# Six merges of probability tiles per unit in another order, and one direct part in the row sums

## The chip, the cores and the metric

The kernel runs on one core of a Trainium2 chip. The metric is the device time of one execution in microseconds (us).

## What is computed

Two identical layers on 2048 tokens of width 1024, in float32. Each is attention with 32 heads of 32 columns, then a routed feed-forward on 8 tokens:

```python
x = x + A(layernorm(x)); x = x + B(layernorm(x))          # twice
# A: q, k, v = split(x @ wqkv); p = softmax(q @ k.T * 32**-0.5); (p @ v) @ wo
# B(y): r = y @ w_r; the 8 tokens with the largest r get
#    y + sigmoid(r) * ((silu(y @ w_gate) * (y @ w_up)) @ w_down), the others y
```

The change lies in the softmax of A: the sums of the exponentials over the keys, by which the outputs are divided.

## The kernel before

Attention of a layer goes through 32 units (NU). A unit is a group of 4 heads (8 groups, NG) and a chunk of 512 queries (4 chunks, QC). Each unit has 16 steps (NT), one for each block of 128 keys. Steps are counted through the layer as `s`; within a unit they are called `kt`.

In a step TensorE makes, in this order: a first half of a row of products of q and k for the row maxima, 25 steps ahead of their use (`pre_mm`, L706; VectorE reduces them, L714); the scores of 128 keys by 512 queries for 4 heads, in two halves (`scores`, L721, into the two PSUM tiles `pre`); the other half of `pre_mm`; and the values matmul of the tile before (`pv_step`, L1043). ScalarE turns the scores into exponentials (L1112). They go to a tile P of 128 x 2048 float32, 1 MB; "tile k" is the P of step k of a unit. P has 9 buffers (PB). In the last 24 steps of a layer no products for maxima are left, and the steps go in threes.

The sum over the keys has two levels. First, the 16 tiles of a unit are added elementwise, in one of three ways:

- `merge(u, a, b)` (L1056): GpSimd issues a DMA that adds tile b onto tile a in SBUF. It needs the exponential of b, and the values matmul of a must have read a. Tile b is free when the DMA has landed.
- `acc_add` (L1053): GpSimd adds a tile into an accumulator `acc` of the unit (the first add takes two tiles). In the last units VectorE does some of it.
- a direct part: the tile is left as it is.

Then `sum_mm` (L1063) makes 8 matmul instructions with a matrix of ones for each part, that is for each direct tile and for the accumulator, which add up over the 128 rows. ScalarE copies the result (L1073), and SyncE stores it.

Each engine has its own queue in the order of the program, and an instruction at the head that waits holds up all behind it. `emit(s, where)` puts the work on the sums into the program, by lists written by hand: in the lists before, `(8, 6)` of MERGED is the merge of tile 7 onto tile 6, put at the end of step 8. Numbers of 16 and more lie in the steps of the next unit. The place only sets the order in the queue; the work starts when the engine gets there and what it needs is done. The sum is put at step 22, the middle of step 6 of the next unit (`SUM_AT`), after the values matmul of tile 5. SyncE loads q for later units at the start of a unit, and keys in the first two units of a group, values in the third, for the next group (`queue_loads`).

A buffer of P that has been released is given to the next new tile; before the first exponential of the tile ScalarE waits for the last use of what lay in the buffer.

Of the kernel before, what the change touches and what calls it, by code (L numbers as in the profile page):

```python
# [19 lines left out]
NT = S // 128  # L20
# [3 lines left out]
NU = NG * QC  # L24
# [9 lines left out]
PB = 9  # L34


MERGED = ((2, 0), (8, 6), (11, 8), (13, 10), (15, 12))
ADDED = ((5, 3), (6, 0), (9, 5), (12, 4), (14, 6), (15, 8), (16, 10), (20, 12))
FIRST = 2
DIRECT = (14, 15)  # L40
LAST_DIRECT = (13, 14, 15)


# [4 lines left out]
KEYS_AT[3, 3] = slice(3 * 512, S)  # L48

ON_DVE = 9


def unit_events(left):

    if left == 0:
        return [(k + 1, "mid", 1, "add", (k, 0 if k == 1 else None, True)) for k in range(1, NT) if k not in LAST_DIRECT]
    ev = [(at, "end", 0, "merge", (k, k + 1)) for at, k in MERGED]
    ev += [(at, "end", 1, "add", (k, FIRST if at == ADDED[0][0] else None, left == 1 and at >= ON_DVE)) for at, k in ADDED]  # L60
    return ev + [(SUM_AT, "mid", 5, "sum", ())]


EVENTS = [unit_events(i) for i in range(3)]


@with_exitstack
def tile_kernel(ctx, tc, x, wqkv, wo, w_r, w_gate, w_up, w_down, out):
# [29 lines left out]
    def ps_st():  # L98
        return banks["now"][1].tile([128, 512], F32, name="st", bufs=1 if banks["wide"] else 3)

    def ps_pre():
        return psum.tile([128, 1024], F32, name="pre", bufs=2)

    def ps_pv():
        return psum.tile([128, 512], F32, name="pv")
# [544 lines left out]
    def layer(n, src, dst, prev=None, following=None):  # L650
# [93 lines left out]
        with ExitStack() as pst:  # L744
# [209 lines left out]
            for k, (c, wb, i) in enumerate(steps):  # L954
# [26 lines left out]
                at = b - (1, 8)[c == 0]  # L981
# [31 lines left out]
        with sbuf(f"at{n}", bufs=2) as aw:  # L1013
            KS[1] = aw.tile([128, 2, 2, S], F32R, name="ks1", bufs=1)
            P, PV, ACC = {}, {}, {}
# [41 lines left out]

            def sum_mm(u):
                p = ps_st()
                parts = [P[u * NT + k] for k in (DIRECT if u < NU - 1 else LAST_DIRECT)] + [ACC.pop(u).rearrange("p (h c) -> p h c", h=4)]  # L1060
                for i, a in enumerate(parts):
                    for h in range(4):
                        pe.matmul(p[32 * h:32 * h + 32, :], ones32, a[:, h, :], start=(i == 0),  # L1063
                                  stop=(i == len(parts) - 1), tile_position=(0, 32 * h))
                return p
# [12 lines left out]
            def sum_out(u):  # L1078
                store_sum(u, sum_mm(u), aw.tile([128, 512], F32, name="sm", bufs=1))
# [13 lines left out]
            def emit(s, where):  # L1093
                u, kt = divmod(s, NT)
                todo = []
                for back in (1, 0):
                    v = u - back
                    if 0 <= v < NU:
                        todo += [(kt + NT * back, pri, fn, args, v) for (k, pos, pri, fn, args) in EVENTS[min(NU - 1 - v, 2)]
                                 if k == kt + NT * back and pos == where]  # L1100
                for k, _, fn, args, v in sorted(todo, key=lambda e: (-e[0], e[1])):
                    fns[fn](v, *args)

            for i in range(4):
# [11 lines left out]
            def rest_of_step(s):  # L1116
                u, kt = divmod(s, NT)
                pr = pre_rows[s + LEAD] if s + LEAD < NS else None
                emit(s, "mid")
                if pr and pr[1] == 15:  # L1120
                    nm_combine(pr[0])
                if (s + LEAD) % NT == 0 and NT <= s + LEAD - NT < NS:
                    nm_row((s + LEAD) // NT - 1)
                emit(s, "end")
                if s == NS + 1:
                    shared["sum"] = sum_mm(NU - 1)
                if s == NS - 20:
                    shared["first"] = aw.tile([128, 512], F32, name="sm", bufs=1)[:, 0:256]
                    sum_load(shared["first"], 0)
                if s == NS - 17:  # L1130
                    recip(shared["first"], 0)
                if s < NS and kt == 0:
                    queue_loads(u)
                    if u == NU - QC:
                        loads.extend((load_wo, a) for a in range(KD))
                if s == (NU - QC) * NT + 1:
                    right.close()
                    shared["wor"] = ExitStack()
                    wop = shared["wor"].enter_context(sbuf(f"wor{n}", side="right"))
                    shared["WOR"] = wop.tile([128, KD, D], F32, name="wor", bufs=1)  # L1140
                if loads:
                    f, *args = loads.pop(0)
                    f(*args)
# [42 lines left out]
        if True:  # L1186
# [81 lines left out]
            for t in range(NT - 2 if n else NT):  # L1268
                oh, ol = OT.pop(t)
                p = ps_pre()  # L1270
# [60 lines left out]
        if n:  # L1331

            parts = ffn.first_rows(rcols)
            waste = ps_pre()
            p = [[waste[:, h] for h in halves], [ps_st(), ps_pv()]]
            (ah, al), (bh, bl) = (OT.pop(t) for t in (NT - 2, NT - 1))
            both = range(2)
            todo = [(i, x, wol, a, both) for i, x in ((0, ah), (1, bh)) for a in range(KD)]
# [99 lines left out]
```

## Time and profile before

| | |
|---|---|
| median of 3 runs | 4543.79 us (4541.69 to 4547.17) |
| the profiled execution | 4545.36 us |
| its span, first to last instruction | 4543.6 us |
| mean granted TensorE clock | 0.996 |
| GpSimd adds into `acc` (L1053) | 422 of 4830 ns, and 62 first ones of 4761 ns |
| merges (L1056) | 310, 1024 KB each, 8.9 us from issue to landing (median) |
| exponentials (L1112) | 2016 of 1022 ns |

The profile is of one execution. An engine's busy share counts its own instructions, without waits. The chain of waits goes back from the last instruction: from each step to what released it, or to the instruction before it on its engine. PE is TensorE's matmul, PEld its weight loads, DVE is VectorE, ACT is ScalarE, POOL is GpSimd, SP is SyncE. A row of a timeline gives the start and the length in us, the engine, the line, the operation, the tile written and those read, how many were joined in the row, and in brackets the idle time of the engine ahead of it with what ended it.

### The profile page before, as it was taken

To read this page: it belongs to the slowest core of one execution; us is meant where nothing else is said; L and a number is where in the kernel's file an instruction comes from. 1 tells how busy PE (TensorE), PEld (TensorE's weight loads), DVE (VectorE), ACT (ScalarE), POOL (GpSimd) and SP (SyncE) were. 2 spreads that over 40 slices of the span, in tenths; PEclk is the share of its full clock that TensorE was granted. 3 is DMA by queue.
4 is the path that set the end of the run, shared out by engine and by line. 5 is a ranking of instruction groups with operands and counts; after the bars stand their busy time and mean duration, and the time that the engine had idled before them with its cause. 6 is when DMAs were issued, how large, how long until landed. Compare 5 with 4: busy or idle time off the path is not lost.

```text
span 4543.6 us, 73545 instructions
## 1 busy us (share of the span) xinstructions
PE 4497.7 (99%) x29241; PEld 2686.0 (59%) x29241; DVE 3156.8 (69%) x4975; ACT 2426.5 (53%) x2574; POOL 3169.1 (70%) x1239
## 2 busy tenths in 40 slices
PE   9999999999999999999999999999999999999998
PEld 7888755555555555548877786554555555555583
DVE  2211588888888888886522225888888888888763
ACT  3322266767676767670222222776767676767600
POOL 4444378989888889835633343898989898889252
PEclk9999999999999999999999999999999999999998
DMA  6757477777777768759698774777768677777598
GB/s 206 209 174 204 135 170 152 174 153 164 162 167 155 173 143 180 169 131 241 183 319 276 253 208 126 168 161 161 170 144 183 148 166 161 167 155 180 145 275 327
DMA packets 329719, 833.62 MB, mean 183 GB/s; under 512 B 43996, under 2 KB 160732, under 8 KB 280206
## 3 DMA queue, kind: packets, MB, share of 16 engines
q1 hardware_dynamic: 275454, 476.43, 35.8%
q0 software_dynamic: 45248, 325.67, 35.4%
q10 hardware_dynamic: 8672, 26.81, 2.3%
q8 instruction: 230, 3.77, 0.3%
q14 instruction: 115, 0.94, 0.1%
HBM read 384.34 MB, written 119.47 MB: 111 GB/s over the span
## 4 chain that ended last, share of the span: by engine, by line
PE 94%; DMA 2%; DVE 2%; issue 1%; POOL 1%; ACT 0%; SPq 0%; ACTq 0%; POOLq 0%; DVEq 0%
PE pv L1043 22%; PE pre L721 21%; PE st L839 17%; PE st L706 16%; PE pre L839 5%; PE pre L1283 5%; PE st L1063 4%; PE pv L549 1%; PE pre L706 1%; PE pv L839 0%; DMA ord<-rd 0%; PE pre L808 0%; DMA wraw<-in_A_wqkv_dram 0%; DVE acc L1053 0%; PE third L721 0%
## 5 line engine op out<-in xcount | busy, mean ns | idle before, releaser
L714 DVE TENSOR_REDUCE nm<-st 128x1 f32<-128x512 f32 x3916 | 2433.6, 684 | 374.7 <-PE st L706 368.8
L1112 ACT ACTIVATE P<-pre 128x1024 f32<-128x1024 f32 x2016 | 1955.2, 1022 | 704.2 <-PE pre L721 515.6
L1053 POOL TENSOR_TENSOR acc<-acc,P 128x2048 f32<-128x2048 f32 x422 | 2038.4, 4830 | 84.3 <-DMA P<-P 74.7
L721 PE MATMUL pre<-q,ks 64*128 64x512 f32 (+1 forms) x8064 | 1117.8, 395 | 1.7 <-ACT P L1112 1.7
L1043 PE MATMUL pv<-P,v 128*32 128x512 f32 x8192 | 1088.4, 605 | 4.5 <-DMA v<-vd 4.5
L706 PEld LDWEIGHTS st<-ks,q 64*128 64x128 f32 x3916 | 546.5, 184 | 906.8 <-DVE nm L714 765.3
L706 PE MATMUL st<-ks,q 64*128 64x512 f32 x3916 | 982.8, 470 | 0.4
L721 PEld LDWEIGHTS pre<-q,ks 64*128 64x128 f32 (+1 forms) x8064 | 765.2, 186 | 162.1 <-ACT P L1112 27.0
L1056 POOL DMA_DIRECT2D P<-P x310 | 294.2, 949 | 279.2 <-PE st L706 184.6
L854 DVE TENSOR_TENSOR lo<-st,hi 128x512 fp32r<-128x512 f32 x128 | 88.4, 691 | 528.0 <-ACT hi L853 507.9
L774 POOL TENSOR_TENSOR ohl<-wraw,ord 128x2048 fp32r<-128x2048 f32 (+1 forms) x54 | 222.5, 4124 | 308.4 <-ACT ord L769 292.7
L774 POOL TENSOR_TENSOR wl<-wraw,wh 128x2048 fp32r<-128x2048 f32 (+1 forms) x54 | 222.6, 4126 | 303.3 <-ACT wh L773 284.4
L853 ACT CAST hi<-st 128x512 fp32r<-128x512 f32 x128 | 75.4, 589 | 490.9 <-PE st L839 488.6
L1043 PEld LDWEIGHTS pv<-P,v 128*32 128x32 f32 x8192 | 163.3, 108 | 265.4 <-issue 258.2
L1053 POOL TENSOR_TENSOR acc<-P 128x2048 f32<-128x2048 f32 x62 | 295.2, 4761 | 11.0 <-ACT P L1112 11.0
L1283 PE MATMUL pre<-woh,ohl 128*128 128x512 f32 x960 | 223.4, 390 | 1.7 <-DVE pre L1316 0.9
L168 POOL TENSOR_TENSOR rs<-mv,eps_c 128x1 f32<-128x1 f32 x64 | 29.2, 456 | 264.7 <-DVE mv L166 264.7
L1283 PEld LDWEIGHTS pre<-woh,ohl 128*128 128x128 f32 x960 | 179.6, 188 | 42.1 <-ACT ohl L1214 2.1
L839 PE MATMUL st<-xh,wh 128*128 128x512 f32 x512 | 201.2, 393 | 0.0
L839 PE MATMUL st<-xh,wl 128*128 128x512 f32 x512 | 199.3, 389 | 0.0
L839 PE MATMUL st<-xl,wh 128*128 128x512 f32 x512 | 199.2, 389 | 0.0
L1214 ACT CAST ohl<-ord 128x1024 fp32r<-128x1024 f32 x32 | 33.6, 1051 | 272.1 <-DVE ord L1205 81.7
(389 smaller groups left out, 4069.0 us busy)
## 6 DMA issues: line engine op xcount, KB each, us to landing
P<-P POOLq DMA_DIRECT2D x310, 1024.0 KB, 8.9
wraw<-in_A_wqkv_dram SPq DMA_DIRECT2D x96, 1024.0 KB
q<-qh SPq DMA_DIRECT2D x256, 128.0 KB
ks<-kh SPq DMA_DIRECT2D x112, 256.0 KB
fw<-in_B_w_down_dram SPq DMA_DIRECT2D x17, 1024.0 KB
vd<-vn SPq DMA_DIRECT2D x32, 512.0 KB
qh<-hi SPq DMA_DIRECT2D x64, 256.0 KB
ql<-lo SPq DMA_DIRECT2D x64, 256.0 KB
```

The costliest lines, as they stand in the source:

```text
L706: pe.matmul(ps[b], Q[u][rows, i, 0, qt * 128:(qt + 1) * 128], KS[(u // QC) % 2][rows, i, 0, j * 512:(j + 1) * 512], start=True, stop=True, ...
L714: dve.tensor_reduce(NM[u][:, j, 2 * i + b:2 * i + b + 1, qt], ps[b], axis=AX.X, op=OP.max, negate=True)
L721: pe.matmul(p[:, b * 512:(b + 1) * 512], KS[(u // QC) % 2][rows, i, slot, kt * 128:(kt + 1) * 128], Q[u][rows, i, slot, :], start=(slot == ...
L774: pool.tensor_tensor(wl[:, sl], raw[:, sl], wh[:, sl].bitcast(F32), op=OP.subtract)
L839: pe.matmul(p, *pair(a, l, r), start=(a == 0 and k == 0), stop=(a == KD - 1 and k == 2))
L854: dve.tensor_tensor(lo, p, hi.bitcast(F32), op=OP.subtract)
L1043: pe.matmul(PV[u][32 * h:32 * h + 32, :], V[g][:, kt, 32 * h:32 * h + 32], P[s][:, h, :], start=(kt == 0), stop=(kt == NT - 1), tile_posit ...
L1053: (dve if on_dve else pool).tensor_tensor(o, a, P[u * NT + k].rearrange("p h c -> p (h c)"), op=OP.add)
L1056: pool.dma_start(P[u * NT + a], P[u * NT + b], accum_op=OP.add)
L1063: pe.matmul(p[32 * h:32 * h + 32, :], ones32, a[:, h, :], start=(i == 0), stop=(i == len(parts) - 1), tile_position=(0, 32 * h))
L1112: act.activation(P[s][:, 2 * i:2 * i + 2, :].rearrange("p h c -> p (h c)"), p, AF.Exp, scale=SCALE)
L1283: pe.matmul(p[:, bl], l[:, a, :], r[a][:, bl], start=(k == 0 and a == 0), stop=(k == 2 and a == KD - 1))
```

## The change

The lists of merges and adds are written anew, as one list with fractions that set the order within a step. There are six merges instead of five: 1 onto 2, 3 onto 4, 8 onto 7, 10 onto 9, 12 onto 13, 15 onto 14. The accumulator takes, in this order, 0 and 5, then 6, 2, 4, 11, 7, 9, 13: eight adds, as before. Tile 14 is the one direct part; before, 14 and 15 were. The last unit but one has a list of its own, with three merges, one GpSimd add and ten adds on VectorE, and tile 15 direct. The last unit stays as it was, with 13, 14 and 15 direct. Where the lists of two units meet in a step, the smaller fraction now goes first; before, the older unit did.

```diff
-MERGED = ((2, 0), (8, 6), (11, 8), (13, 10), (15, 12))
-ADDED = ((5, 3), (6, 0), (9, 5), (12, 4), (14, 6), (15, 8), (16, 10), (20, 12))
-FIRST = 2
-DIRECT = (14, 15)
+SUMS = (
+    (3, "merge", 2, 1), (5, "merge", 4, 3), (6, "add", 0, 5), (7, "add", 6), (9, "merge", 7, 8), (9.5, "add", 2), (11, "merge", 9, 10),
+    (11.5, "add", 4), (12, "add", 11), (14, "merge", 13, 12), (14.5, "add", 7), (16, "merge", 14, 15), (16.5, "add", 9), (19.5, "add", 13))
+DIRECT = (14,)
+
+BEHIND_SUMS = (
+    (3, "merge", 2, 1), (5, "merge", 4, 3), (6, "add", 0, 5), (7, "vadd", 6), (8, "vadd", 2), (9.5, "vadd", 9), (10, "merge", 8, 7), (11, "vadd", 4),
+    (11.5, "vadd", 10), (12, "vadd", 11), (13, "vadd", 12), (14, "vadd", 8), (15, "vadd", 13), (16, "vadd", 14))
+BEHIND_DIRECT = (15,)
 LAST_DIRECT = (13, 14, 15)
...
-ON_DVE = 9
...
-    ev = [(at, "end", 0, "merge", (k, k + 1)) for at, k in MERGED]
-    ev += [(at, "end", 1, "add", (k, FIRST if at == ADDED[0][0] else None, left == 1 and at >= ON_DVE)) for at, k in ADDED]
+    ev = []
+    for at, what, k, *other in (SUMS, BEHIND_SUMS)[left == 1]:
+        args = (k, *other) if what == "merge" else (k, *(other or [None]), what == "vadd")
+        ev.append((int(at), "end", at % 1, "merge" if what == "merge" else "add", args))
     return ev + [(SUM_AT, "mid", 5, "sum", ())]
...
-                parts = [P[u * NT + k] for k in (DIRECT if u < NU - 1 else LAST_DIRECT)] + [ACC.pop(u).rearrange("p (h c) -> p h c", h=4)]
+                parts = [P[u * NT + k] for k in (LAST_DIRECT, BEHIND_DIRECT, DIRECT)[min(NU - 1 - u, 2)]] + [ACC.pop(u).rearrange("p (h c) -> p h c", h=4)]
...
-                for k, _, fn, args, v in sorted(todo, key=lambda e: (-e[0], e[1])):
+                for k, _, fn, args, v in sorted(todo, key=lambda e: (e[1], -e[0])):
                     fns[fn](v, *args)
```

## The prediction

> **What bounds the kernel now.** I read the busy shares first, then the chain of waits, then one unit of the attention stage (layer 0, the unit whose first values matmul starts at 941.16) on TensorE, ScalarE and GpSimd.
>
> ```profile
> PE 4497.7 (99%) x29241; PEld 2686.0 (59%) x29241; DVE 3156.8 (69%) x4975; ACT 2426.5 (53%) x2574; POOL 3169.1 (70%) x1239
> PE 94%; DMA 2%; DVE 2%; issue 1%; POOL 1%; ACT 0%; SPq 0%; ACTq 0%; POOLq 0%; DVEq 0%
> ```
> The second line is the chain that ended last: TensorE carries 94% of it. So work taken from TensorE's queue in the attention stage shortens the kernel, as long as nothing makes TensorE wait instead. The stretches of that unit (length, then busy time of PE, PEld, DVE, ACT, POOL, the granted clock, the DMA share) say how near the others are:
>
> ```profile
> 941.16:986.93 45.77, 45.77 (x345) 23.17 (x344) 40.12 (x67) 32.08 (x35) 39.84 (x14) 1.00 0.78 167
> 951.16:961.16 10.00, 10.00 (x82) 4.44 (x80) 7.26 (x13) 6.34 (x7) 6.29 (x2) 1.00 0.02 4
> 971.16:986.93 15.77, 15.77 (x120) 8.29 (x112) 14.48 (x24) 11.62 (x13) 14.43 (x6) 1.00 1.05 225
> ```
> One unit takes 45.77 us, and TensorE is busy for all of it. GpSimd (39.84) and VectorE (40.12) are close behind. The DMA engines are full at the unit's end (1.05) and idle around its sum (0.02).
>
> **The term that goes.** The chain inside the unit (start, us, what) and the groups of instructions (count | busy us, mean ns | idle before):
>
> ```profile
> 954.73 1.00 PE pv L1043 x8
> 955.73 2.58 PE st L1063 x24
> 958.30 0.43 PE st L706 x2
> ```
> ```profile
> L1063 PE MATMUL st<-P,ones 128*32 128x512 f32 x1040 | 123.3, 592 | 0.0
> L1063 PE MATMUL st<-acc,ones 128*32 128x512 f32 x512 | 66.7, 592 | 2.0 <-DVE acc L1053 2.0
> ```
> The sum of a unit is 24 matmul instructions, 8 for each of its three parts: tile 14, tile 15, the accumulator. It stands on the chain with 2.58 us, so a part costs 2.58 / 3 = 0.86. By busy time a part costs 123.3 / (1040 / 8) = 0.95; I take 0.86, since neighbouring matmuls overlap and the chain counts only what each adds, and keep 0.95 as the other end. The change drops one part in every unit but the last of a layer: 31 x 2 = 62 parts. 62 x 0.86 = 53.3 us (58.9 by the other end).
>
> **What it costs GpSimd.** Let t = 0 be 941.16, where the values matmul of tile 0 starts.
>
> ```profile
> 941.16 1.07 PE L1043 MATMUL pv<-P,v 128*32 128x512 f32 x8
> 942.50 1.10 PE L721 MATMUL pre<-q,ks 64*128 64x512 f32 x8
> 943.86 1.07 PE L1043 MATMUL pv<-P,v 128*32 128x512 f32 x8
> 959.93 1.06 PE L1043 MATMUL pv<-P,v 128*32 128x512 f32 x8
> ```
> ```profile
> 942.81 0.87 POOL L1056 DMA_DIRECT2D P<-P  x1 [0.46 <-PE st L706]
> 943.43 4.88 POOL L1053 TENSOR_TENSOR acc<-acc,P 128x2048 f32<-128x2048 f32 x1
> 947.98 4.87 POOL L1053 TENSOR_TENSOR acc<-P 128x2048 f32<-128x2048 f32 x1
> 952.93 4.60 POOL L1053 TENSOR_TENSOR acc<-acc,P 128x2048 f32<-128x2048 f32 x1
> 961.58 0.87 POOL L1056 DMA_DIRECT2D P<-P  x1 [4.06 <-PE st L706]
> 966.98 0.92 POOL L1056 DMA_DIRECT2D P<-P  x1
> 972.40 0.96 POOL L1056 DMA_DIRECT2D P<-P  x1
> 977.80 1.01 POOL L1056 DMA_DIRECT2D P<-P  x1
> ```
> A step is 943.86 - 941.16 = 2.70. The fourth TensorE row is the values matmul of tile 6, the first after the sum (t = 18.77). A merge is issued 1.65 after the values matmul of its destination starts (942.81 - 941.16; 961.58 - 959.93). From a merge to the next add are 0.62, from merge over one add to merge 5.40 (961.58 to 966.98), from add to add 4.55 to 4.95. A merge with two adds behind it so takes 0.62 + 4.95 + 4.78 = 10.35, where 4.78 is 5.40 - 0.62.
>
> Both orders have eight adds per unit; the new one has six merges for five: + 0.62 for GpSimd. The unit becomes 45.77 - 0.86 = 44.91. GpSimd's new order, in t:
> - Merge 2<-1 needs the values matmul of tile 2 (5.40): 5.40 + 1.65 = 7.05. Behind it in GpSimd's queue waits the add of 13 of the unit before, the last into its accumulator; it ends at 12.45. TensorE wants that accumulator for the second part of the sum, at 955.73 - 941.16 + 0.86 = 15.4: 2.9 to spare.
> - Merge 4<-3: ready at 10.80 + 1.65 = 12.45, reached at 12.45. Adds 0+5 and 6.
> - Merge 7<-8 at 22.80 (ready near 22.3), add 2; merge 9<-10 at 28.20, adds 4 and 11; merge 13<-12 at 38.55 (ready 38.5), add 7; merge 14<-15 at 43.95, add 9 until 49.35.
> - The next unit's 2<-1 is due at 44.91 + 7.05 = 51.96: GpSimd idles 2.6 us per unit. It keeps up, with all its idle time at that one merge. Cost on the path: none while eight adds do not grow by 2.6 us together.
>
> VectorE's 40.12 of 44.91 leaves it hidden. The sixth merge is one more DMA of 1 MB per unit; by the windows above the DMA engines are free around the sum, which is where 2<-1 and 4<-3 now move.
>
> **What it costs the buffers.** A released P buffer goes to the next new tile in the order in which the last uses stand in the program; it is no fixed ring. By that order the new program gives tile 7 the buffer of 1, tile 9 that of 3, tile 3 of the next unit that of 12, tile 6 of the next that of 15. These four are set free by a merge's landing. All buffers that an add sets free come at least 5 us early (tile 2: add over at 28.2, its buffer wanted by tile 14 near 36). When the exponentials start (ScalarE):
>
> ```profile
> 940.53 1.94 ACT L1112 ACTIVATE P<-pre 128x1024 f32<-128x1024 f32 x2 [0.27 <-PE pre L721]
> 954.03 1.94 ACT L1112 ACTIVATE P<-pre 128x1024 f32<-128x1024 f32 x2 [0.76 <-PE pre L721]
> 959.28 1.94 ACT L1112 ACTIVATE P<-pre 128x1024 f32<-128x1024 f32 x2 [0.33 <-PE pre L721]
> 964.70 1.94 ACT L1112 ACTIVATE P<-pre 128x1024 f32<-128x1024 f32 x2 [0.76 <-PE pre L721]
> 983.63 1.94 ACT L1112 ACTIVATE P<-pre 128x1024 f32<-128x1024 f32 x2 [0.79 <-ACT P L1112]
> 991.73 1.94 ACT L1112 ACTIVATE P<-pre 128x1024 f32<-128x1024 f32 x2 [0.77 <-PE pre L721]
> ```
> They are tiles 1, 6, 7, 9, and 0 and 3 of the next unit. Less 0.86 for those behind the sum, tile 7 starts at t = 17.26, tile 9 at 22.68, tile 3 at 49.71; tile 6 of the next unit at 12.87 + 44.91 = 57.78. So the merges may take, from issue to landing: 2<-1 10.2 us (17.26 - 7.05), 4<-3 10.2 (22.68 - 12.45), 13<-12 11.2 (49.71 - 38.55), 14<-15 13.8. Today the tightest has 16.5 (merge at 1.65, exponential of tile 7 at 18.12). A late exponential costs TensorE nothing for the first 0.5: tile 1 is done at 942.47, and the half of the scores that needs it starts at about 942.50 + 0.55.
>
> Landings over all 310 merges (min/median/max), and of the single ones issued at 942.81, 961.58, 972.40 and 977.80:
>
> ```profile
> DMA to landing us min/median/max: 6.9/8.9/14.6
> DMA to landing us min/median/max: 9.0/9.0/9.0
> DMA to landing us min/median/max: 7.8/7.8/7.8
> DMA to landing us min/median/max: 12.2/12.2/12.2
> DMA to landing us min/median/max: 14.5/14.5/14.5
> ```
> 7.8 is a merge with little beside it, 9.0 one beside the loads of q that start with the unit, 12.2 and 14.5 two merges 5.40 apart beside the loads of keys, in the full stretch. The nearest rows for 2<-1 and 4<-3, which lie just behind the loads of q and in the empty stretch, are 7.8 and 9.0: they land at 14.9 to 16.1 and 20.3 to 21.5, in time. For 13<-12 the next merge ahead is 10.35 before it instead of 5.40, so its transfer need not queue behind another: I take 9.0 (in time), with 14.5 as the bad end.
>
> The Trainium skill ("DMA: Bandwidth & Descriptors", Anatomy of one DMA) gives 2.0 us plus the bytes at 436 GB/s, an estimate of 4.4 us for 1 MB. The trace disagrees: no merge here lands before 6.9. By the page's figure every merge would be twice as early as needed and the landing rival below would have no chance.
>
> **The end of a layer.** The last unit but one gets ten VectorE adds for six.
>
> ```profile
> L1053 DVE TENSOR_TENSOR acc<-acc,P 128x2048 f32<-128x2048 f32 x34 | 77.6, 2291 | 32.9 <-DMA P<-P 28.8 <-POOL acc L1053 2.0
> 1997.51 4.51 DVE acc L1053 x2
> ```
> Four more at 2.29 are 9.2 us per layer; VectorE waits for merges there for 28.8 / 2 = 14.4 us per layer, which the three merges of the new order mostly avoid, so they fit. The second row is on the chain: the last add of that unit stands behind two or three of the last unit's on VectorE, and the sum waits for it (the 2.0 us in the group of L1063 above). In the new order that add comes at step 16, ahead of them: - 2.0 us for both layers, or 0 if VectorE is late.
>
> **Sum.** Profiled execution 4545.4 (span 4543.6) - 53.3 - 2.0 = 4490.1. It lies 1.6 above the median of the runs, 4543.8; so 4488.5 in their terms.
>
> **The rivals.**
> 1. *Late landing of 13<-12 in some units.* For: today's fourth merge takes 14.5 in a unit that loads keys (28 units: two of four in each group, but for the last group of a layer). Against: the wider spacing. If it took 12.2 to 14.5 there, tile 3 would be 0.5 to 2.8 late beyond the slack, 1.65 in the middle: 46 us, most of the gain: 4535. Milder forms lie between 4500 and 4535; with the units that load values it could be 4545. Chance 0.13.
> 2. *Slower: 2<-1 and 4<-3 land late in every unit.* Place: exponentials of tiles 7 and 9. For: 2<-1 comes 8 us behind 14<-15, which shares the DMA engines with the loads of q. It decides from 10.2 + 0.5 + 0.86 = 11.6 us of landing on. At 12.2 the unit loses 0.64 net, 40 us in all: 4584. Against: the stretch after t = 10 has a DMA share of 0.02. Chance 0.07.
> 3. *Slower: the buffers go round as a ring of nine.* Tile 0 of the next unit (983.63, t = 41.61 in the new unit) would wait for the add of 7, over at 43.95: 2.34 - 0.5 late, less 0.86, 1.0 per unit: 4605. I read the order otherwise. Chance 0.04.
> 4. *GpSimd becomes the bound.* This needs adds longer by 2.6 / 8 = 0.33 us.
>
> ```profile
> L1053 POOL TENSOR_TENSOR acc<-acc,P x422: 4565/4891/5387, 588.8 to 4209.6; 128x2048 f32<-128x2048 f32 x141
> ```
> A mean of 5.2 would add 0.37 x 8 - 2.6 = 0.3 per unit, 20 us: 4509. Against: adds in the full stretch took no more than 5.00. Chance 0.05.
>
> That the change drops less than it says can be excluded: the list of direct parts of all but the last unit has one entry.
>
> **The numbers.** My forecast, 4488.5, has 0.71. Its own range is 4482 (a part at 0.95) to 4500. The range of 8 in 10 takes in rival 4 and the milder half of rival 1: 4480 to 4522. What a measurement here tells from no change is about 0.2%, 9 us. Faster: 0.71 + 0.05 + 0.07 of rival 1 = 0.83. Slower: rivals 2 and 3 and a little of 1, 0.12. Same: 0.05.
>
> **What would show it.** Right: the sum on the chain at 1.72 us with 16 matmuls, L1063 at 544 instead of 1040 on P, units of 44.9 us, GpSimd waiting only for TensorE at 2<-1, and ScalarE never waiting for a merge. Wrong: "ACT P" waiting for DMA P<-P or for POOL acc (rivals 1 to 3), TensorE waiting for the accumulator at the sum, or GpSimd without a gap (rival 4).

## The result and the profile after

The changed kernel takes 4505.08 us (median of 4 runs, 4503.45 to 4506.12), the kernel before 4543.88 beside it (4541.69 to 4547.17). The ratio is 0.9912, with a 95% interval of 0.9899 to 0.9924. So 38.8 us are gone, of 55.3 forecast. The profiled execution took 4506.12 (span 4504.2).

The busy shares and the chain that ended last, from the page of the changed kernel:

```profile
PE 4448.4 (99%) x28745; PEld 2674.4 (59%) x28745; DVE 3175.5 (71%) x4983; ACT 2426.1 (54%) x2574; POOL 3214.2 (71%) x1293
PE 93%; DMA 3%; DVE 2%; issue 1%; POOL 1%; ACT 0%; SPq 0%; ACTq 0%; POOLq 0%; DVEq 0%
```

TensorE has 496 instructions fewer (29241 - 28745), which is 62 parts of 8, and still carries the chain; the share of DMA on it went from 2% to 3%. The sums of two units on the chain (start, us, what), and GpSimd over one unit whose first values matmul starts at 934.90:

```profile
904.51 1.72 PE st L1066 x16
949.48 1.72 PE st L1066 x16
```
```profile
941.97 0.88 POOL L1059 DMA_DIRECT2D P<-P  x1 [2.56 <-PE st L709]
942.58 4.88 POOL L1056 TENSOR_TENSOR acc<-acc,P 128x2048 f32<-128x2048 f32 x1
947.36 0.95 POOL L1059 DMA_DIRECT2D P<-P  x1
957.50 0.89 POOL L1059 DMA_DIRECT2D P<-P  x1
962.66 1.19 POOL L1059 DMA_DIRECT2D P<-P  x1
973.39 0.88 POOL L1059 DMA_DIRECT2D P<-P  x1 [0.26 <-PE st L709]
978.53 1.20 POOL L1059 DMA_DIRECT2D P<-P  x1
```

A sum is 1.72 instead of 2.58. The next one starts 949.48 - 904.51 = 44.97 later; over most of the layer this period is 44.93, and in the kernel before it was 45.80 (both worked out from the starts of the sums). The merges come 7.07, 12.46, 22.60, 27.76, 38.49 and 43.63 after the start of the unit.

The same unit and its second quarter, as stretches (length, then busy time of PE, PEld, DVE, ACT, POOL, the granted clock, the DMA share, GB/s):

```profile
934.90:979.84 44.94, 44.94 (x338) 22.90 (x337) 40.11 (x67) 32.11 (x35) 41.96 (x15) 1.00 0.95 200
944.90:954.90 10.00, 10.00 (x82) 4.84 (x79) 8.02 (x15) 6.43 (x8) 9.92 (x4) 1.00 0.94 195
```

TensorE is busy without a gap. But the DMA engines went from 0.78 to 0.95 of a unit, and the stretch 10 to 20 us behind its start, which had a share of 0.02, now has 0.94.

Up to the last units of a layer all is as forecast. Then, once in each layer, comes a unit with a period of 54.80 (the first) and 54.14 (the second). TensorE at the first of them:

```profile
1893.77 1.04 PE L1066 MATMUL st<-acc,ones 128*32 128x512 f32 x8
1899.08 0.76 PE L709 MATMUL st<-ks,q 64*128 64x512 f32 x1 [4.27 <-DMA q<-qh]
1902.18 0.76 PE L709 MATMUL st<-ks,q 64*128 64x512 f32 x1 [2.34 <-DMA sd<-sm]
```

In brackets is TensorE's idle time. The products that wait are the first for the row maxima of the layer's last unit; what they need is that unit's q, which SyncE loads only in steps 0 to 5 of the unit in which this happens, the last but two. The second wait is put down to a store of the sums, which these products don't read. In the second layer the trace names q for both waits, 3.92 us and then

```profile
4128.42 0.76 PE L709 MATMUL st<-ks,q 64*128 64x512 f32 x1 [2.57 <-DMA q<-qh]
```

The periods are 9.87 and 9.21 longer than 44.93: 19.1 us in the profiled execution. This is the loss that the forecast doesn't have. The gain falls short by only 16.5 us, because the end of a layer gained more than forecast (below), and because the stretch from the last sum of the first layer to the first sum of the second, in which the change drops one part only, also differs from run to run (859.7 us in the kernel before, 855.2 here, 855.2 to 860.1 in the other runs with five or six merges).

SyncE's issues ahead of the stall, in the kernel before and then in the changed one:

```profile
1889.66 7.47 SPq L96 DMA_DIRECT2D wor<-in_A_wo_dram  x7
1902.55 6.02 SPq L96 DMA_DIRECT2D q<-qh  x4
1910.50 5.55 SPq L96 DMA_DIRECT2D q<-ql  x2
```
```profile
1859.28 6.51 SPq L99 DMA_DIRECT2D wor<-in_A_wo_dram  x7
1878.14 2.13 SPq L99 DMA_DIRECT2D q<-qh  x4
1880.37 4.16 SPq L99 DMA_DIRECT2D q<-ql  x2
```

In both, seven loads of wo go out together, after the row-maxima transfers let SyncE go on, and the q loads follow. In the kernel before, the products that need this q start without a wait, 4 us after its last issue ended (1910.50 + 5.55). In the changed kernel the last issue ended at 1880.37 + 4.16 = 1884.53, some 10 us before TensorE wanted this q, and that was not enough. The products of the kernel before:

```profile
1919.06 1.04 PE L1063 MATMUL st<-acc,ones 128*32 128x512 f32 x8
1920.03 0.50 PE L706 MATMUL st<-ks,q 64*128 64x512 f32 x2
```

The stretches from the issues of wo on, before and then after:

```profile
1885.00:1905.00 20.00, 20.00 (x154) 10.70 (x151) 18.27 (x30) 14.39 (x16) 19.40 (x7) 1.00 1.03 249
1905.00:1921.00 16.00, 16.00 (x126) 7.74 (x124) 12.60 (x22) 10.29 (x11) 13.33 (x4) 1.00 0.91 265
```
```profile
1860.00:1880.00 20.00, 20.00 (x152) 10.26 (x146) 18.31 (x30) 14.97 (x16) 19.62 (x8) 1.00 1.02 268
1880.00:1900.00 20.00, 15.57 (x117) 7.40 (x113) 12.80 (x22) 10.28 (x11) 17.36 (x6) 0.95 1.05 248
```

Both are full when wo goes out. Before, the engines have room again (0.91) while q comes in; after, they are still full (1.05). Whether it is this that makes q late, the experiments have to tell.

### The profile page after: what moved, and what is told of

It is laid out like the page before. It is cut to its first block, busy times and chain, and to the rows that moved or that the text cites. A ratio compares the mean times of both kernels' runs of the same rounds, so it can differ in the third digit from the quotient of the medians.

```text
span 4504.2 us, 72867 instructions
## 1 busy us (share of the span) xinstructions
PE 4448.4 (99%) x28745; PEld 2674.4 (59%) x28745; DVE 3175.5 (71%) x4983; ACT 2426.1 (54%) x2574; POOL 3214.2 (71%) x1293
## 3 DMA queue, kind: packets, MB, share of 16 engines
q0 software_dynamic: 53312, 384.39, 43.2%
q1 hardware_dynamic: 275454, 476.43, 35.5%
## 4 chain that ended last, share of the span: by engine, by line
PE 93%; DMA 3%; DVE 2%; issue 1%; POOL 1%; ACT 0%; SPq 0%; ACTq 0%; POOLq 0%; DVEq 0%
PE pv L1046 23%; PE pre L724 21%; PE st L842 17%; PE st L709 16%; PE pre L842 6%; PE pre L1286 4%; PE st L1066 2%; PE pv L552 1%; PE pre L709 1%; DMA ord<-rd 1%; PE pv L842 1%; PE pre L811 0%; DMA q<-qh 0%; PE third L724 0%; DVE ord L1208 0%
## 5 line engine op out<-in xcount | busy, mean ns | idle before, releaser
L1056 POOL TENSOR_TENSOR acc<-acc,P 128x2048 f32<-128x2048 f32 x420 | 2052.0, 4886 | 9.4
L1059 POOL DMA_DIRECT2D P<-P x366 | 364.3, 995 | 268.3 <-PE st L709 244.3
L1056 POOL TENSOR_TENSOR acc<-P 128x2048 f32<-128x2048 f32 x62 | 307.4, 4957 | 0.0
```

The lines of the kernel that those rows point to most:

```text
L1056: (dve if on_dve else pool).tensor_tensor(o, a, P[u * NT + k].rearrange("p h c -> p (h c)"), op=OP.add)
L1059: pool.dma_start(P[u * NT + a], P[u * NT + b], accum_op=OP.add)
```

## The experiments

Each was timed beside the kernel before on the same chip, which took 4547.30 us on one chip (wo at `NU - 2`, five merges, old order with six), 4545.81 on another (the last two runs) and 4543.80 on a third (the others). So runs on different chips are compared by their ratios. The edits are to the changed kernel unless said otherwise.

**Move the loads of wo.** First to the last unit but one, behind the last loads of q:

```diff
-                    if u == NU - QC:
+                    if u == NU - 2:
```

> The changed kernel, with the eight loads of wo queued at the start of the last unit but one of a layer instead of the first unit of the last group. Theory A (the loads of q for the last unit come late, because eight loads of 512 KB and six merges a unit fill the DMA engines just ahead of them, and TensorE waits for q at the first products for maxima of the last unit): the wait of some 9 to 10 us goes in both layers, 4505 becomes 4485 to 4488, and no period between sums is over 46 us. Theory B (the stall at the layer's end comes from the new list of the last unit but one, through VectorE): nothing changes, 4503 to 4507.

4493.31 us (4490.22 to 4496.69); ratio 0.9876 (0.9861 to 0.9892). The wait for q is gone and every period is 44.93 until the layer's end. But the last period but one is 39.88 in the first layer and 36.63 in the second, for 34.91 and 34.95 in the changed kernel. TensorE and SyncE there:

```profile
1960.20 1.34 PE L724 MATMUL pre<-q,ks 33*128 33x512 f32 x2 [1.31 <-DMA q<-nmx]
```
```profile
1945.36 7.46 SPq L99 DMA_DIRECT2D nmx<-nmr  x4
1958.21 1.18 SPq L99 DMA_DIRECT2D q<-nmx  x2
```

The row maxima of the last unit, which go out to DRAM and back into q, now stand behind wo. So the move took away the wait for the loads of q and made a new one, for the row maxima. The same move in the kernel before:

> The kernel before, with the same move of the loads of wo. Theory A: with five merges a unit q came just in time, so there is nothing to gain: 4542 to 4546. Theory B: the same. If instead it gains 5 us or more, the kernel before was paying for that collision too, and the changed kernel's gain is smaller by that than the direct part's price says.

4554.68 us (4550.41 to 4557.23); ratio 1.0013 (1.0004 to 1.0022), so some 6 us slower than before, which the expectation didn't have. Its trace shows no wait of TensorE for the row maxima; the last period but one is longer in both layers (38.37 and 39.58 us for 37.19 and 36.93, between the starts of the accumulator's part), and what makes it so is not shown. Now one unit earlier, so that the row maxima don't stand behind wo, in the changed kernel and in the kernel before:

```diff
-                    if u == NU - QC:
+                    if u == NU - 3:
```

> The changed kernel, with the loads of wo queued one unit later than in the changed kernel, behind the last unit's loads of q (the last unit but two). Theory A (the missing time is q coming late behind the loads of wo): every period between sums 44.9 us up to the last two, the last ones 34.9 and 23.8 as in the changed kernel, no wait for DMA at the products for maxima: 20 us under the changed kernel, 4484 to 4488, a ratio to the kernel before near 0.987. If wo only collides with something else there, as it did with the row maxima's way through memory when it was put into the last unit but one, the gain is less than 17.

> The kernel before with the same move. Theory A: nothing to gain, ratio 0.998 to 1.002, periods of 45.8. The difference to the run with the changed lists is then what the change brings without the collision: the forecast says 55 us.

Changed kernel with the move: 4489.24 us (4488.67 to 4490.55); ratio 0.9881 (0.9866 to 0.9896). Kernel before with the move: 4542.57 (4541.32 to 4547.55); ratio 0.9999 (0.999 to 1.0008). SyncE in the first of the two:

```profile
1879.52 4.48 SPq L99 DMA_DIRECT2D q<-qh  x4
1884.04 2.49 SPq L99 DMA_DIRECT2D q<-ql  x2
1905.55 5.47 SPq L99 DMA_DIRECT2D wor<-in_A_wo_dram  x7
```

The loads of q go out alone, wo 20 us later. All periods are 44.93 up to the last two (34.95 and 23.75). The expectation's mark for a second collision, a gain under 17, is met by the medians (15.8), but the trace shows no such collision: between the first and the last sum of the two layers 18.95 us are gained, and outside them 3.4 are lost again, 2.7 of these between the layers. In time this place of wo and the one before it can't be told apart (ratios of 0.9881 and 0.9876); in the traces the last two periods of both layers together are 6.65 us shorter here. So the move is worth 14 to 16 us with six merges (by the ratios 0.9881 and 0.9912, or by the medians) and nothing with five, and without the collision the new lists bring 4542.57 - 4489.24 = 53 us.

**The new order without the sixth merge:**

```diff
-    (11.5, "add", 4), (12, "add", 11), (14, "merge", 13, 12), (14.5, "add", 7), (16, "merge", 14, 15), (16.5, "add", 9), (19.5, "add", 13))
-DIRECT = (14,)
+    (11.5, "add", 4), (12, "add", 11), (14, "merge", 13, 12), (14.5, "add", 7), (16.5, "add", 9), (19.5, "add", 13))
+DIRECT = (14, 15)
```

> The changed kernel without the merge of tile 15 onto 14: five merges a unit in the new order, tiles 14 and 15 direct again (the last unit but one keeps its new list). Tells the order apart from the sixth merge. If the whole gain is the direct part's 8 matmul instructions: periods of 45.8 us and 4538 to 4544, a little under the kernel before for the new end of the layer (2 x 2 us), and no wait for q at the layer's end, since the DMA engines carry as much as before. If the order itself is worth something, it is faster than 4536. If the q wait comes from where the merges lie and not from their number, it shows here too: about 4555.

4542.98 us (4539.14 to 4546.79); ratio 0.999 (0.9981 to 0.9999). The periods are 45.80, and there is no q wait. In the ordinary units the order by itself brings nothing. What is left, some 4 us with an interval that reaches almost to nothing, fits the last two periods of the two layers: 117.42 us together, for 121.98 in the kernel before. That is the new list of the last unit but one, with its one direct part.

**The sixth merge without the new order** (an edit to the kernel before):

```diff
-MERGED = ((2, 0), (8, 6), (11, 8), (13, 10), (15, 12))
+MERGED = ((2, 0), (8, 6), (11, 8), (13, 10), (15, 12), (16, 14))
-DIRECT = (14, 15)
+DIRECT = (14,)
```

> The kernel before with a sixth merge, 15 onto 14, put at step 16 ahead of the add of 10, and tile 14 as the one direct part; the old order otherwise. If the order does not matter: the same 4503 to 4507 as the changed kernel, with periods of 44.9 us. If it does (the sixth merge joins a stretch in which the DMA engines are already full, the adds of 10 and 12 wait longer for their merges, and GpSimd falls behind): periods above 45.3 us, 4520 or more, with GpSimd waiting for DMA for more than the 75 us of the kernel before.

4524.77 us (4521.94 to 4527.15); ratio 0.9948 (0.9935 to 0.9962). Its waits (total us, times, longest), and TensorE in the longest ordinary unit:

```profile
POOL acc L1053 <- DMA P<-P: 137.3, 85, 3.4
...
PE st L706 <- DMA q<-qh: 16.7, 11, 6.1
```
```profile
3462.34 0.86 PE L706 MATMUL st<-ks,q 64*128 64x512 f32 x2 [1.25 <-DMA q<-qh]
```

Periods run from 44.91 to 46.53, with 53.17 and 53.79 at the last q. In the old order GpSimd waits for landings, but in the trace TensorE's matmuls never wait for GpSimd's accumulator. What they wait for is q, 11 times: twice at the last q, and once in each of nine ordinary units, all with periods over 45.4. So this is the same collision, at more places. By the ratios (0.9948 and 0.9912) the new order is worth 16 us once there are six merges. The traces put some 12 of them into the ordinary units (56 periods of 45.15 on average, for 44.93 in the changed kernel) and 3.7 into the last two periods of the layers (121.09 together, for 117.40).

**A seventh merge**, on top of the move of wo to `NU - 3`, to see where the DMA engines end. Tile 5 goes onto 6, no tile is direct, and the sum of ordinary units stands two steps later. The new `SUMS`:

```diff
+    (3, "merge", 2, 1), (5, "merge", 4, 3), (7, "merge", 6, 5), (8, "add", 2, 0), (9, "merge", 7, 8), (9.5, "add", 4), (11, "merge", 9, 10),
+    (11.5, "add", 6), (12, "add", 11), (14, "merge", 13, 12), (14.5, "add", 7), (16, "merge", 14, 15), (16.5, "add", 9), (19.5, "add", 13), (21.5, "add", 14))
+DIRECT = ()
-    return ev + [(SUM_AT, "mid", 5, "sum", ())]
+    return ev + [(SUM_AT + (2 if left == 2 else 0), "mid", 5, "sum", ())]
```

> The same place for wo, with a seventh merge, 5 onto 6, no direct part at all, eight adds (0 with 2, then 4, 6, 11, 7, 9, 13, 14) and the sum two steps later. TensorE then has 8 matmul instructions for a unit's sum, a period of 44.1 if nothing else binds: 4433. The DMA share of the changed kernel in this stage is 0.90 of a 44.9 us unit; one more merge at about 5 us of all 16 engines needs 45.5 us of a 44.1 us unit. So I expect the DMA engines to bind: periods of 45.5 or more, 4520 or slower, with GpSimd waiting for merges to land. If it comes under 4470, the DMA engines have more room than their share says.

4548.98 us (4536.68 to 4576.26); ratio 1.0028 (1.0011 to 1.0045). The same stretch of the first layer before, after, and with seven merges, and then TensorE's waits for q with seven:

```profile
600.00:1850.00 1250.00, 1250.00 (x9392) 631.61 (x9388) 1095.91 (x1803) 876.18 (x929) 1120.42 (x358) 1.00 0.75 163
```
```profile
600.00:1850.00 1250.00, 1250.00 (x9350) 636.65 (x9350) 1115.73 (x1836) 892.50 (x947) 1168.05 (x391) 1.00 0.90 189
```
```profile
600.00:1850.00 1250.00, 1216.72 (x8936) 622.10 (x8935) 1092.80 (x1798) 873.55 (x927) 1166.06 (x410) 0.98 0.97 208
```
```profile
PE st L709 <- DMA q<-qh: 48.7, 14, 9.7
```

The total came out as expected, in another form: no steady loss per unit, but quiet units of 44.06 and eleven of 48 to 56, in nine of which the trace has TensorE wait for q; GpSimd's adds wait for landings for only 8.0 us in all. At a DMA share of 0.97 the collision that the changed kernel has once in a layer comes four or five times.

**The old rule of order within a step**, on the changed kernel:

```diff
-                for k, _, fn, args, v in sorted(todo, key=lambda e: (e[1], -e[0])):
+                for k, _, fn, args, v in sorted(todo, key=lambda e: (-e[0], e[1])):
```

> The changed kernel with the old order of two units' work in one step (the older unit first). It meets only at step 3: the add of 13 of the unit before goes ahead of merge 2<-1 instead of behind it. By the reckoning of the prediction GpSimd has idle time there, the add ends at 9.2 and the merge goes out at 9.2 instead of 7.05, its landing near 18 is before the exponential of tile 8 at 20.0 that takes the buffer: the same time as the changed kernel, 4503 to 4507, ratio 0.991. If the buffer of 1 were wanted by tile 7 (17.3), as the prediction had it, units would lose about 0.5 us: 4530.

4486.37 us (4485.02 to 4487.65); ratio 0.9875 (0.986 to 0.989). This was a miss, and it has the lowest median of all, below both kernels. GpSimd and TensorE at the place of the stall:

```profile
1883.88 4.59 POOL L1056 TENSOR_TENSOR acc<-acc,P 128x2048 f32<-128x2048 f32 x1 [1.01 <-DMA P<-P]
1888.40 0.87 POOL L1059 DMA_DIRECT2D P<-P  x1
```
```profile
1893.62 1.04 PE L1066 MATMUL st<-acc,ones 128*32 128x512 f32 x8
1894.59 0.50 PE L709 MATMUL st<-ks,q 64*128 64x512 f32 x2
```

The add of 13 goes ahead of merge 2<-1 of the next unit, so that merge is issued at 1888.40, while in the changed kernel it went out at 1885.58. The products start right behind the sum: no q wait, and all periods are 44.93 up to the last two. The engines are as full there as in the changed kernel (a share of 1.02 from 1860 to 1880 and 1.05 from 1880 to 1895). So full engines alone don't make the wait: some 3 us in the time of one merge decide it.

**Both cures at once** (the old rule, wo at `NU - 3`), and the changed kernel once more beside it:

> Both at once: the old sort of the run before and the loads of wo behind the last unit's loads of q. If both cured one and the same thing (the last unit's q late behind a merge and the loads of wo), the second cure has nothing left to gain: 4484 to 4489, ratio 0.987 to 0.9885. If they cured two things of 15 us each, it is 4468 to 4474.

> The changed kernel itself once more, beside it on the same chip: ratio 0.990 to 0.9925, some 15 to 18 us above the run with both moves, and in its trace a period of 54 us between two sums near the end of each layer, TensorE waiting there for q.

4488.22 us (4486.89 to 4489.16), ratio 0.9873 (0.9857 to 0.989); and 4504.66 (4502.1 to 4509.94), ratio 0.9908 (0.9892 to 0.9925), with the long periods at 54.40 and 54.49. The two cures don't add up: they take away the same wait, and it is worth 16 us by the medians (4504.66 - 4488.22).

## Why the prediction was right, and where it missed

**The term that goes** was right: 0.86 per part on the chain, 1.72 with 16 matmuls. The period fell by 45.80 - 44.93 = 0.87, and without the collision the kernel is 53 us (by the move) to 57 us faster (4543.8 - 4486.37, by the old rule), against 55.3.

**GpSimd's timeline** held within 0.5 us at every merge (7.05, 12.45, 22.80, 28.20, 38.55, 43.95 forecast). The add of 13 ended at 942.58 + 4.88, t = 12.56, with 2.9 to spare as forecast. The idle time was 2.56 at 2<-1, and 0.26 at 13<-12, where none was foreseen.

**The buffers** were read wrongly in three of four, without harm. By the program's own order as built, the buffer of 1 goes to tile 8, that of 3 to tile 12, that of 12 to tile 4 of the next unit; only tile 6 of the next from 15 was right. The three true allowances are longer than those forecast. The landings of all merges, and every wait of ScalarE between 600 and 1890:

```profile
DMA to landing us min/median/max: 7.0/8.8/14.7
```
```profile
ACT P L1115 <- PE pre L724: 232.4, 318, 1.1
ACT P L1115 <- ACT P L1115: 84.9, 113, 0.8
ACT sm L1076 <- PE st L1066: 43.6, 28, 1.6
ACT P L1115 <- ACT o L1071: 7.1, 29, 0.3
```

No exponential waits for a merge or for an add. Rivals 1 to 3 all needed that and are out. For rival 4 the adds would have to take 5.2; the mean of the 420 went from 4830 to 4886 ns.

```profile
L1056 POOL TENSOR_TENSOR acc<-acc,P 128x2048 f32<-128x2048 f32 x420 | 2052.0, 4886 | 9.4
```

**The tail** was forecast at -2.0. The last two periods went from 37.19 and 23.93 to 34.91 and 23.76 in the first layer, from 36.93 and 23.93 to 34.95 and 23.78 in the second: together -4.6. Of this 1.7 are the parts that go there, so the list is worth 2.9.

**The range** held partly by luck. 4505.08 lies beyond the forecast's own range (4482 to 4500). It lies within 4480 to 4522 only because that range had made room for rival 4 and for the milder half of rival 1, and neither came.

**The step that failed** is "the sixth merge is one more DMA of 1 MB per unit; by the windows above the DMA engines are free around the sum". That was true of one ordinary unit before, and it was used up: its 0.02 became 0.94. What I left out is that the same engines carry SyncE's loads, and that these have little to spare somewhere. The trace of before shows the place: in the last group the loads of wo go out, q for the last unit follows them and is in use 4 us after its last issue ended. With the sixth merge 10 us were too few. All four rivals asked whether an exponential, an accumulator or GpSimd would wait; none asked whether TensorE would wait for a load. The term missing from the sum is 16 us in the runs (4504.66 - 4488.22).

What stays open is which packets go first. In the 20 us from 1860 on SyncE's queue moved 3.08 MB in the changed kernel and 3.38 under the old rule, at full engines in both; the table of queues from 1890 to 1900, in the changed kernel (packets, MB, share of 16 engines):

```profile
q0 software_dynamic: 249, 1.91, 91.7%
q1 hardware_dynamic: 280, 0.43, 15.1%
```

q0 carries the merges, q1 SyncE's loads. While TensorE waits for q, the merges take six times the share of the loads. The Trainium skill ("DMA: Bandwidth & Descriptors", Queues, rings and completion order) says that a DMA engine serves the queues that have work in turn and empties a whole packet of one before it goes on to the next. The near equal counts in these rows, 249 and 280, with packets of 7.7 KB for the merges and 1.5 KB for the loads, would agree with that if the profile's packets are the ones meant. From 1880 to 1890 the counts are 208 to 869, but 691 of the 869 fall into the 2 us from 1888, in which the merges moved only 23; from 1880 to 1888 they are 185 to 178. Under the old rule they are 196 to 364 from 1880 to 1888. So the loads get ahead in the gaps between merges, and beside a merge they are held near one packet for one in the changed kernel's rows. That is a reading of counts and no proof: no run here varied the size of a packet.

## What to carry to other kernels

A transfer that is added to a busy loop is to be costed in two places: in the loop, and at each place where another queue's load has its least lead, which is often where a stage begins or ends. Read the DMA share of the whole loop, not that of the gap into which the transfer moves. Here it was 0.75 with five merges, 0.89 to 0.90 in the new order with six, where the collision came or didn't depending on what goes out when, and 0.97 with seven, where it came in many units. And when such a collision shows, move the load or shift the transfer: here either was worth about a third of what the change brings.

## What the runs showed of the hardware

A wait of TensorE cost more than its length. The stall was 4.27 + 2.34 = 6.61 us of idle time, but the unit became 9.87 longer; in the second layer 3.92 + 2.57 = 6.49 made it 9.21 longer. The stretches behind the wait (the number ahead of the DMA share is the granted clock):

```profile
1895.00:1900.00 5.00, 0.76 (x1) 0.28 (x1) 0.12 (x1) 0.46 (x1) 4.92 (x2) 0.78 1.05 231
1900.00:1905.00 5.00, 2.82 (x11) 1.94 (x11) 1.54 (x3) 1.11 (x2) 1.05 (x1) 0.50 0.21 49
1905.00:1910.00 5.00, 5.00 (x31) 1.86 (x30) 3.32 (x7) 2.38 (x3) 0.00 (x0) 0.69 0.02 2
1910.00:1920.00 10.00, 10.00 (x80) 5.56 (x80) 9.22 (x16) 7.13 (x8) 9.31 (x4) 1.00 0.79 159
```

The clock fell to 0.50 and came back by 1910. Lost clock in these rows is 0.22 x 5 + 0.50 x 5 + 0.31 x 5 = 5.2 us, part of which lies in the wait itself; the 3.3 that the waits leave unexplained fit into the rest, by this estimate. With wo at `NU - 2` a wait of 1.31 was followed by a granted clock of 0.57 and 0.75 in the two stretches of 5 us from 1960 on, and that period was 4.97 longer than in the changed kernel.

A merge costs the DMA engines more for its bytes than the transfers on SyncE's queue do. The software queue was busy for 43.2% of 4504.2 us with 366 merges, an estimate of 5.3 us of all 16 engines for each, or 5.1 us per MB; SyncE's queue moved 476.43 MB in 35.5%, 3.4 us per MB. Six merges make 32 us of a unit of 44.93 before anything is loaded.

```profile
q0 software_dynamic: 53312, 384.39, 43.2%
```
